# A two-layer kernel whose second layer follows the first at a distance of three units in place of two

## The chip, the cores and the metric

The kernel runs on one core of one Trainium2 chip. The metric is the device time of one execution in microseconds (us). The kernel before was run three times: 2016.63 us median, from 2016.15 to 2020.16. The profiled execution took 2016.63 us, and its trace spans 2014.8 us from the first to the last instruction.

The engines, by their names in the rows: PE is TensorE (matrix products; PEld its weight loads), DVE is VectorE, ACT is ScalarE, SP is SyncE, which here only issues transfers (its queue is SPq). Each engine takes its own instructions strictly in the order in which the program lists them and holds the next one until its semaphores allow it.

## The reference

For 2 sequences of 6080 steps and 256 channels, a gated scan, then two feed-forward blocks on the 12160 resulting rows:

```
f = lb + (1 - lb) * sigmoid(f_logit);  h = f * h + (1 - f) * x;  y[t] = h
z   = relu(y @ w_in1) ** 2 @ w_out1          # 256 -> 2048 -> 256
out = elu(z @ w_in2) @ w_out2                # 256 -> 2048 -> 256
```

The four weight matrices arrive as 64-bit floats.

## The kernel before

**Units.** The 12160 rows are cut into 12 units: unit 0 of 512 + 384 rows, all others of 512 + 512 (`units_of`). Each unit goes through the first layer (scan, `w_in1`, relu and square, `w_out1`) and, later, through the second (`w_in2`, elu, `w_out2`). The first layer's result of a unit goes to a buffer in HBM (`xd`) and is loaded back as `F1` when the second layer takes the unit up.

**Order of the units.** Lines 229 to 232 write down the list `runs` of (layer, unit). With `BEHIND = 2` it is (0,0) (0,1) (1,0) (0,2) (1,1) (0,3) ... (1,9) (0,11) (1,10) (1,11), with layer 0 for the first and 1 for the second. A stage, below, is one entry of this list.

**Slots.** A stage has 8 slots, one for each eighth of the hidden width. All products are made of three matmuls on a split of each number into a high and a low part (function `three`). In units 0 and 1 of the first layer (the "plain" stages) the two halves of the rows take 16 slots of 12 matmuls for `w_in` (into c0 and c1 or c2 and c3, by turns) and 12 for `w_out`. All other stages save an eighth of the first product by sums of blocks: a slot has 9 matmuls ("first", on tile `xa`), 12 ("later", on tile `xb`) and twice 12 for `w_out` ("out", L858), 45 in all. Each out needs one tile `g`, whose low part is the DVE instruction L681. So L681 comes 16 times in each stage, and counts the slots on DVE; the out that uses a `g` is issued some 8 us of planned time after its slot. L681 number 17 to 32 belong to (0,1), 33 to 48 to the third stage.

**What must stand before a stage.** (0,u) needs its rows scanned: in four quarters, each with loads of `fs` and `xs` (SP, L569, four issues each, two buffers each), one ACT instruction (L573), and on DVE two transposes (L578), two L584, L592, two scans (L605) and L610. The result is tile `F0`, one buffer. Then `add_parts` makes `xa` and `xb` (one buffer each) from `F0`, or from `F1` for the second layer, with L518 and L485, L488.

**Weights.** During the first two or three stages DVE and ACT also turn the 64-bit weights into high and low parts. `make` prepares a slot of `w_in` (for the second layer with four sums L319 to L322 and L342 and stores to `wd`), `out` a slot of `w_out`, and `sums` (`add_sums`) reloads a slot of `w_in1` from `rd` (SP, L455, tile `a<-rd`) and makes the sums that the 45-matmul slots of the first layer need. Their planned times are spread by lines 932 to 936: `make` and `out` of the second layer up to the start of (1,0), `sums` up to the start of (0,2).

**Order of instructions.** The class `Order` collects all steps with a cost in us and a due time, runs a list scheduler on these planned costs, and issues each engine's instructions in the resulting order. So the order on every engine is fixed when the program is built.

Of the kernel before, what the change touches and what calls it, by code (L numbers as in the profile page):

```python
# [18 lines left out]
SIZES = ((512, 384), (512, 512))  # L19
LEAD = 2  # L20
GAP = 56
BEHIND = 2
AGE = 8.0
ROW = 1 / 2240
START = 12.0
# [126 lines left out]
def kernel(  # L152
# [66 lines left out]
    def slots_of(m, u):  # L219

        if not plain(m, u):
            return [(m, u, None, g) for g in range(KG)]
        a, b = ([(m, u, h, g) for g in range(KG)] for h in range(2))
        got = a[:LEAD]
        for i in range(LEAD, KG + LEAD):
            got += a[i : i + 1] + b[i - LEAD : i - LEAD + 1]
        return got

    runs = [(0, u) for u in range(BEHIND)]
    for u in range(BEHIND, NU):  # L230
        runs += [(1, u - BEHIND), (0, u)]
    runs += [(1, u) for u in range(NU - BEHIND, NU)]
    slots = [s for r in runs for s in slots_of(*r)]
# [729 lines left out]
    for kind, s in pe_order:  # L963
# [4 lines left out]
        if kind != "later" and s == first_of[m, u]:  # L968
            if m == 0:
                keys = {}  # L970
                before = slots_of(0, u - 1)
                for hh in range(2):
                    due = in_due[(m, u, hh, 0) if plain(m, u) else s]
                    for q in range(2):
                        k = before[SCANS[2 * hh + q] * len(before) // KG] if u >= BEHIND else None
                        keys[hh, q] = add_scan(n_scan, u, hh, q, due - 6.0 + 2.0 * (q - 1), n_first[k] if k else None)
# [43 lines left out]
```

## Time and profile before

| | |
|---|---|
| median of 3 runs | 2016.63 us |
| profiled execution, its span | 2016.63 us, 2014.8 us |
| PE, DVE, ACT busy | 97%, 83%, 81% of the span |
| PE idle, waiting for `xa` | 35.0 us in 2 waits (one is the start of the program) |
| stages in the trace: (0,1) ends, (1,0) from and to, (0,2) begins in earnest | 181.57; 181.57 to 261.63; 282.77 us |

A row of the timeline has start and duration in us, the engine, the line, the tiles written and read, the count, and in brackets the idle time before it with what ended it. "x9" is nine instructions merged to one row.

### The profile page before, as it was taken

To read this page: it belongs to the slowest core of one execution; us is meant where nothing else is said; L and a number is where in the kernel's file an instruction comes from. 1 tells how busy PE (TensorE), PEld (TensorE's weight loads), DVE (VectorE), ACT (ScalarE), POOL (GpSimd) and SP (SyncE) were. 2 spreads that over 40 slices of the span, in tenths; PEclk is the share of its full clock that TensorE was granted. 3 is DMA by queue.
4 is the path that set the end of the run, shared out by engine and by line. 5 is a ranking of instruction groups with operands and counts; after the bars stand their busy time and mean duration, and the time that the engine had idled before them with its cause. 6 is when DMAs were issued, how large, how long until landed. Compare 5 with 4: busy or idle time off the path is not lost.

```text
span 2014.8 us, 24509 instructions
## 1 busy us (share of the span) xinstructions
PE 1964.0 (97%) x8688; PEld 1630.8 (81%) x8688; DVE 1674.3 (83%) x2285; ACT 1638.0 (81%) x2170; POOL 0.2 (0%) x4
## 2 busy tenths in 40 slices
PE   5999969999999999999999999999999999999998
PEld 4987958888888888888888888888888888888886
DVE  7877998888889879879888888987987988857886
ACT  6987968888888888888788788888888878878886
POOL 0000000000000000000000000000000000000000
PEclk9999989999999999999999999999999999999999
DMA  7877644324424334333432442433433333233231
GB/s 202 241 243 244 215 138 138 128 85 144 133 102 144 102 134 133 113 134 108 139 132 85 138 130 101 144 102 134 133 113 134 113 113 133 92 108 116 100 109 57
DMA packets 235138, 267.30 MB, mean 133 GB/s; under 512 B 160008, under 2 KB 160776, under 8 KB 235016
## 3 DMA queue, kind: packets, MB, share of 16 engines
q1 hardware_dynamic: 234432, 265.21, 41.3%
q8 instruction: 68, 1.11, 0.2%
q10 hardware_dynamic: 584, 0.53, 0.1%
q14 instruction: 54, 0.44, 0.1%
HBM read 221.91 MB, written 43.78 MB: 132 GB/s over the span
## 4 chain that ended last, share of the span: by engine, by line
PE 88%; DVE 4%; ACT 3%; DMA 2%; issue 1%; SPq 1%; ACTq 0%; DVEq 0%
PE a L858 47%; PE c L636 41%; DVE g L681 1%; DMA a<-rd 1%; DMA fs<-in_f_logit_dram 1%; ACT g L676 1%; ACT r L728 1%; ACT r L661 1%; SPq L569 0%; ACT a L372 0%; DVE a L378 0%; ACT st L375 0%; DVE a L381 0%; DMA st<-in_moe_w_in_dram 0%; DVE F L605 0%
## 5 line engine op out<-in xcount | busy, mean ns | idle before, releaser
L858 PE MATMUL a<-g,wo 128*128 128x512 f32 (+1 forms) x4608 | 1098.6, 387 | 0.9 <-DVE g L681 0.9
L858 PEld LDWEIGHTS a<-g,wo 128*128 128x128 f32 x4608 | 864.8, 188 | 173.8 <-DVE g L681 1.3
L681 DVE TENSOR_TENSOR g<-r,g 128x1024 fp32r<-128x1024 f32 (+2 forms) x384 | 463.4, 1207 | 157.5 <-ACT g L676 156.7
L636 PE MATMUL c<-xb,ws 128*128 128x512 f32 (+2 forms) x2208 | 525.7, 387 | 0.0
L676 ACT ACTIVATE g<-r 128x1024 fp32r<-128x1024 f32 (+2 forms) x384 | 403.4, 1051 | 110.0 <-PE a L858 91.6
L636 PEld LDWEIGHTS c<-xb,ws 128*128 128x128 f32 x2208 | 413.9, 188 | 82.2
L636 PE MATMUL c<-xa,ws 128*128 128x512 f32 (+1 forms) x1680 | 419.3, 393 | 43.0 <-ACT xa L485 35.0
L636 PEld LDWEIGHTS c<-xa,ws 128*128 128x128 f32 x1680 | 316.9, 190 | 114.6 <-ACT xa L485 35.4
L759 ACT ACTIVATE s<-c 128x512 f32<-128x512 f32 (+1 forms) x528 | 306.4, 586 | 5.5 <-PE c L636 4.7
L671 DVE SCALAR_TENSOR_TENSOR r<-e,r 128x1024 f32<-128x1024 f32 (+1 forms) x192 | 232.2, 1209 | 32.2 <-ACT e L668 32.1
L665 ACT ACTIVATE e<-r 128x1024 f32<-128x1024 f32 (+1 forms) x192 | 201.7, 1050 | 44.3 <-DVE r L803 41.4
L661 ACT ACTIVATE r<-r 128x1024 f32<-128x1024 f32 x192 | 201.6, 1050 | 2.4
L668 ACT ACTIVATE e<-e 128x1024 f32<-128x1024 f32 (+1 forms) x192 | 201.4, 1049 | 1.5
L799 ACT ACTIVATE r<-c 128x512 f32<-128x512 f32 (+1 forms) x176 | 104.0, 591 | 94.7 <-PE c L636 94.7
L763 DVE TENSOR_TENSOR s<-s 128x512 f32<-128x512 f32 (+1 forms) x176 | 119.9, 681 | 71.0 <-ACT s L759 70.9
L796 DVE TENSOR_TENSOR s<-c,s 128x512 f32<-128x512 f32 (+1 forms) x176 | 120.5, 685 | 27.1 <-PE c L636 24.5
L807 DVE TENSOR_TENSOR r<-c,s 128x512 f32<-128x512 f32 (+1 forms) x176 | 119.7, 680 | 4.4
L803 DVE TENSOR_TENSOR r<-c,s 128x512 f32<-128x512 f32 (+1 forms) x176 | 120.0, 682 | 2.2
L810 DVE TENSOR_TENSOR r<-s 128x512 f32<-128x512 f32 (+1 forms) x176 | 119.5, 679 | 0.0
L655 ACT ACTIVATE r<-r 128x1024 f32<-128x1024 f32 x80 | 84.3, 1054 | 3.8 <-DVE r L810 3.8
L658 ACT ACTIVATE r<-r 128x512 f32<-128x512 f32 x80 | 50.4, 630 | 35.8 <-DVE r L803 35.0
L605 DVE TENSOR_TENSOR_SCAN F<-fT,carry,xT 128x256 f32<-128x256 f32 (+2 forms) x94 | 65.4, 724 | 1.2
(47 smaller groups left out, 759.0 us busy)
## 6 DMA issues: line engine op xcount, KB each, us to landing
ws<-wd SPq DMA_DIRECT2D x176, 896.0 KB, 4.9
fs<-in_f_logit_dram SPq DMA_DIRECT2D x184, 64.0 KB, 2.1
xs<-in_x_dram SPq DMA_DIRECT2D x184, 64.0 KB, 2.2
xd<-o SPq DMA_DIRECT2D x46, 256.0 KB, 4.4
F<-xd SPq DMA_DIRECT2D x22, 512.0 KB, 4.6
out_dram<-o SPq DMA_DIRECT2D x88, 128.0 KB, 2.3
st<-in_moe_w_out_dram SPq DMA_DIRECT2D x16, 512.0 KB, 5.6
wd<-wp SPq DMA_DIRECT2D x24, 256.0 KB, 3.5
```

Of the source, the lines that this page charges most:

```text
L636: nc.tensor.matmul(out, lhsT=ws[:, p, w], rhs=xs[:, r, v], start=start and q == 0, stop=stop and q == 2, skip_group_check=check,)
L661: nc.scalar.activation(r_t[0], r_t[0], AF.Square)
L665: nc.scalar.activation(t["e"], r_t[0], AF.Relu, scale=-1.0)
L668: nc.scalar.activation(t["e"], t["e"], AF.Exp, scale=-1.0)
L671: nc.vector.scalar_tensor_tensor(r_t[0], t["e"], 1.0, r_t[0], op0=ALU.subtract, op1=ALU.max)
L676: nc.scalar.activation(g_t[s, which][:, 0], r_t[0], AF.Copy)
L681: nc.vector.tensor_tensor(g_t[s, which][:, 1], r_t[0], g_t[s, which][:, 0].bitcast(F32), op=ALU.subtract)
L759: nc.scalar.activation(t["s"][:, c - 1], t[c], AF.Copy)
L763: nc.vector.tensor_tensor(t["s"][:, 1], t["s"][:, 1], t["s"][:, 2], op=ALU.add)
L796: nc.vector.tensor_tensor(t["s"][:, 0], t[0], t["s"][:, 0], op=ALU.add)
L803: nc.vector.tensor_tensor(odd[0][:, 1], t[2], t["s"][:, 0], op=ALU.add)
L858: nc.tensor.matmul(a, lhsT=y, rhs=v, start=begin and jj == 0 and p == 0, stop=end and jj == len(mine) - 1 and p == 2, skip_group_check=True,)
```

## The change

One number. With `BEHIND = 3` the list `runs` is (0,0) (0,1) (0,2) (1,0) (0,3) (1,1) ... (0,11) (1,9) (1,10) (1,11).

```
-BEHIND = 2
+BEHIND = 3
```

All else follows from the planner. The scans of unit 2 and the `sums` of the first layer now have to stand before the third stage, which is (0,2); the second layer's weights have until the fourth. The condition `u >= BEHIND` at L975 drops the hold that tied the scans of unit 2 to slots of unit 1. The tiles' sizes and the filler tile of `GAP` = 56 floats ahead of the weight buffers are the same in both kernels. The number of instructions on each engine is the same.

On DVE, the kernel before ends the scan of unit 2 (tile F0_2514) here, between the L681 number 45 and 46 (g_2656, g_2663) of (1,0):

```order
L584 TENSOR_SCALAR fT_2665<-fT_2665,ga_59,gb_60 128x256
L681 TENSOR_TENSOR g_2656<-r_2519,g_2656 128x2x448
L584 TENSOR_SCALAR fT_2665<-fT_2665,ga_59,gb_60 128x256
L807 TENSOR_TENSOR r_2683<-c3_2565,s_2555 128x448
L592 SCALAR_TENSOR_TENSOR xT_2661<-fT_2665,xT_2661 128x512
L810 TENSOR_TENSOR r_2683<-s_2555 128x448
L605 SCALAR_TENSOR_TENSOR F0_2514<-fT_2665,carry_61,xT_2661 128x256
L681 TENSOR_TENSOR g_2663<-r_2549,g_2663 128x2x448
L605 SCALAR_TENSOR_TENSOR F0_2514<-fT_2665,carry_61,xT_2661 128x256
L671 SCALAR_TENSOR_TENSOR r_2645<-e_2659,r_2645 128x2x448
L610 COPY carry_61<-F0_2514 128x2
L518 TENSOR_TENSOR F0_2514<-F0_2514 128x512
```

The changed kernel ends the same scan (tile F0_1548) around L681 number 26 (g_1708) of (0,1):

```order
L578 STREAM_TRANSPOSE xT_1684<-xs_1624 128x8x2x32
L578 STREAM_TRANSPOSE fT_1695<-fs_1602 128x8x2x32
L610 COPY carry_61<-F0_1548 128x2
L584 TENSOR_SCALAR fT_1695<-fT_1695,ga_59,gb_60 128x256 x2
L592 SCALAR_TENSOR_TENSOR xT_1684<-fT_1695,xT_1684 128x512
L605 SCALAR_TENSOR_TENSOR F0_1548<-fT_1695,carry_61,xT_1684 128x256
L681 TENSOR_TENSOR g_1708<-r_1575,g_1708 128x1024
L378 SCALAR_TENSOR_TENSOR a_1711<-a_1711,st_1658 128x512
L605 SCALAR_TENSOR_TENSOR F0_1548<-fT_1695,carry_61,xT_1684 128x256
L381 SCALAR_TENSOR_TENSOR a_1711<-st_1658,a_1711 128x512
L610 COPY carry_61<-F0_1548 128x2
L518 TENSOR_TENSOR F0_1548<-F0_1548 128x512
```

In the first list the scan's end stands beside L681 number 46, that is at the 14th of 16 slots of its stage, in the second at the 10th.

On SP, the loads of unit 2 stand before the change among the weight loads (L475) of (1,0), with reloads from `rd` and `xd` between them:

```order
L569 DMA xs_2476<-in_x_dram 32x8x64 x4
L455 DMA a_2496<-rd6_168 128x512
L918 DMA F1_2390<-xd1_171 128x1024
L475 DMA ws_2525<-wd0_0_146 128x2x896
L569 DMA fs_2559<-in_f_logit_dram 32x8x64 x4
L569 DMA xs_2580<-in_x_dram 32x8x64 x4
L475 DMA ws_2622<-wd0_1_147 128x2x896
L569 DMA fs_2640<-in_f_logit_dram 32x8x64 x4
```

After the change they stand among the stores of weights (L345, L346) and the reloads for `sums` of (0,1):

```order
L569 DMA xs_1424<-in_x_dram 32x8x64 x4
L472 DMA ws_1449<-wd0_6_152 128x2x512
L345 DMA wd0_3_149<-wp_1438 128x512
L346 DMA wd0_3_149<-a_1419 128x512
L569 DMA fs_1478<-in_f_logit_dram 32x8x64 x4
L569 DMA xs_1502<-in_x_dram 32x8x64 x4
L455 DMA a_1524<-rd4_166 128x512
L569 DMA xs_1527<-in_x_dram 32x8x64 x4
L345 DMA wd1_2_156<-wp_1517 128x512
L346 DMA wd1_2_156<-a_1466 128x512
L345 DMA wd1_2_156<-wp_1546 128x512
L346 DMA wd1_2_156<-a_1519 128x512
```

A load behind an L345 or L346 is not issued before DVE or ACT has made what that store takes.

## Rows read from the trace of the kernel before

**Rows 1.** The page: the span, busy times, granted clock in 40 slices.
```profile
span 2014.8 us, 24509 instructions
PE 1964.0 (97%) x8688; PEld 1630.8 (81%) x8688; DVE 1674.3 (83%) x2285; ACT 1638.0 (81%) x2170; POOL 0.2 (0%) x4
PEclk9999989999999999999999999999999999999999
```

**Rows 2.** Timeline of PE where (0,2) begins.
```profile
261.63 0.40 PE L636 MATMUL c<-xa,ws 128*128 128x512 f32 x1
...
278.23 0.79 PE L636 MATMUL c<-xa,ws 128*128 128x512 f32 x1 [15.13 <-ACT xa L485]
280.48 2.50 PE L636 MATMUL c<-xa,ws 128*128 128x512 f32 x5 [1.46 <-DVE xa L488]
282.77 3.10 PE L858 MATMUL a<-g,wo 128*128 128x448 f32 x12
285.71 2.91 PE L636 MATMUL c<-xb,ws 128*128 128x512 f32 x12
```

**Rows 3.** Two stretches of DVE: length, busy (count), clock, DMA share, GB/s.
```profile
107.87:164.42 56.55, 41.42 (x76) 1.00 0.77 243
182.04:280.34 98.30, 93.45 (x154) 0.91 0.61 187
```

**Rows 4.** Groups of DVE in 182.04:280.34: busy, mean ns of one, idle before.
```profile
L681 DVE TENSOR_TENSOR g<-r,g 128x896 fp32r<-128x896 f32 (+1 forms) x17 | 18.8, 1105 | 0.0
L319 DVE TENSOR_TENSOR a<-a 128x128 f32<-128x128 f32 x4 | 1.2, 289 | 3.8 <-DMA a<-rd 3.8
```

**Rows 5.** Timeline of DVE, a scan and what follows it at once.
```profile
263.36 0.74 DVE L605 TENSOR_TENSOR_SCAN F<-fT,carry,xT 128x256 f32<-128x256 f32 x1
264.02 1.06 DVE L671 SCALAR_TENSOR_TENSOR r<-e,r 128x896 f32<-128x896 f32 x1
```

**Rows 6.** Timeline of PE, two slots apart by 45 matmuls in (1,1).
```profile
361.76 2.20 PE L636 MATMUL c<-xa,ws 128*128 128x512 f32 x9
...
371.96 2.20 PE L636 MATMUL c<-xa,ws 128*128 128x512 f32 x9
```

**Rows 7.** Timeline of PE from (0,1) to (1,0).
```profile
178.85 2.88 PE L858 MATMUL a<-g,wo 128*128 128x512 f32 x12
181.57 0.77 PE L636 MATMUL c<-xa,ws 128*128 128x448 f32 x3
...
185.31 1.49 PE L636 MATMUL c<-xa,ws 128*128 128x448 f32 x3 [1.55 <-ACT r L728]
186.60 3.73 PE L858 MATMUL a<-g,wo 128*128 128x512 f32 x12
...
204.07 2.90 PE L858 MATMUL a<-g,wo 128*128 128x512 f32 x12
206.81 1.99 PE L636 MATMUL c<-xa,ws 128*128 128x448 f32 x9
...
215.93 1.99 PE L636 MATMUL c<-xa,ws 128*128 128x448 f32 x9
```

**Rows 8.** Timeline of DVE: L681 number 22 and 28.
```profile
141.65 1.23 DVE L681 TENSOR_TENSOR g<-r,g 128x1024 fp32r<-128x1024 f32 x1 [1.30 <-ACT g L676]
...
173.63 1.22 DVE L681 TENSOR_TENSOR g<-r,g 128x1024 fp32r<-128x1024 f32 x1
```

**Rows 9.** Waits of DVE for the reloads of `sums`.
```profile
DVE a L319 <- DMA a<-rd: 11.2, 5, 3.8
```

**Rows 10.** Page, DMA issues: KB each and median us to landing; all packets.
```profile
DMA packets 235138, 267.30 MB, mean 133 GB/s; under 512 B 160008, under 2 KB 160776, under 8 KB 235016
fs<-in_f_logit_dram SPq DMA_DIRECT2D x184, 64.0 KB, 2.1
```

**Rows 11.** Chain of waits: start, us, a load of `fs` in it.
```profile
261.29 4.63 DMA fs<-in_f_logit_dram
```

**Rows 12.** Stage (0,1), all engines: length, PE, PEld, DVE, ACT, POOL, clock, DMA.
```profile
94.50:181.57 87.07, 87.07 (x396) 73.34 (x394) 67.64 (x123) 72.64 (x113) 0.00 (x0) 1.00 0.79 257
```

## The prediction

> **What bounds the kernel now.** I read the page first: PE is busy for 97% of the span and its clock is at full speed in all slices but one [rows 1]. So the time is PE's work plus the few places where PE has none, and a change of order can only act there. The timeline of PE shows two such places after the start of the program. From 282.77 us to the end I leave it alone: every stage transition there is an old one of the kind that the changed kernel has as well, and at (1,1) PE goes over without a gap [rows 6].
>
> The large gap is at the start of (0,2) [rows 2]. PE begins its nine "first" matmuls at 261.63 and issues the next out at 282.77. A slot of 45 matmuls of 512 columns takes 371.96 - 361.76 = 10.20 us [rows 6], 0.227 each, so nine take 2.04, and the out should start at 263.67: 19.1 us are lost. After it the twelve matmuls from 282.77 to 285.71 take 2.94 where twelve take 2.72, and five of the first ones took 2.50, half speed; with what that slowed out adds (at 448 columns it should have taken 2.43) the loss is 19.6 us. The wait is for `xa`, that is for the scans of unit 2.
>
> The small one is from (0,1) to (1,0) [rows 7]: from the first matmul at 181.57 to the out at 204.07 there are two firsts and two laters of 448 columns and three outs of 512. At 9.12 us for a slot of 448 (215.93 - 206.81) this is 16.7 us in place of 22.5: 5.8 us lost, most of it to waits for ACT and to matmuls that run slower behind them.
>
> Why is `xa` late for (0,2)? DVE. From 182.04, where it writes `xb` of (1,0), to 280.34, where `xa` of (0,2) is done, it is busy for 93.45 of 98.30 us [rows 3]: it is full, and PE has only 74.1 us of matmuls in (1,0) (8 x 9.12, and four outs of 512 columns still from the plain stage, 0.29 more each). So (1,0) asks DVE for more than PE lasts, and the difference is the gap.
>
> **The change, step by step.** I count the instructions of DVE between fixed points of its list in both kernels, and price each kind by its mean in the trace, less 0.08 us, since in a full queue the next one starts before the recorded end: L605 has 0.74 and its successor starts 0.66 later [rows 5]. The means are L681 1.105, L319 0.289 and so on [rows 4].
>
> Check on before: from `xb` of (1,0) to `xa` of (0,2) its list has 151 instructions: 17 L681 (17.6 us), 16 L671 (16.0), 40 L763 to L810 (21.1), the 32 of unit 2's scans (15.5: per quarter two transposes 1.22, two L584 0.66, L592 0.60, two L605 1.32, L610 0.07), 39 for weights (15.2) and 7 for parts (5.6). Sum 91.0, where 93.45 were measured as busy. So the counting is good to some 3%.
>
> Now the changed kernel by stages:
> - (0,1), from `xb` of unit 1 to the last of `xa` for (0,2): 109 instructions, 55.7 us (12 L681 13.5, scans 32 15.5, weights 59 22.0, parts 6 4.7). In the trace the first point is at 107.87 and PE wants (0,2) at 181.57: 73.7 us. In the part of it up to 164.42 DVE was busy for 41.42 of 56.55 [rows 3], and the list gains 15.5 of scans there and loses 6.7 of weights.
> - (0,2), from `xb` of (0,2) to `xb` of (1,0): 143 instructions, 82.2 us (16 L681 18.3, 39 of L763 to L810 23.6, weights 63 25.0, scans 14 7.0, parts 11 8.3). PE has 8 x 10.20 = 81.6.
> - (1,0), to `xb` of (0,3): 103 instructions, 69.1 us, for 74.1 of PE.
>
> Nothing disappears: scans and weights are the same number of instructions. But the work with an early due time is now spread over three stages, each about as long as PE's, where before one stage of 74.1 us had to hold 91. `xa` and `xb` of each next stage stand before L681 number 13 and 14 of the stage under way, while (0,2) had its `xb` done only beside number 15 and 16.
>
> *The term that goes*: -19.6.
>
> *The transition out of (0,1)* stays one, now to (0,2). PE's list is the same in form, c1 to c3 are released by the same late relus on ACT, and DVE makes the same kind of parts. Its price lies between 0 (as at (1,1), rows 6) and the 21.1 us of [rows 2]; nearest is the 5.8 it costs today [rows 7], so nothing changes: +0.
>
> *A jam inside (0,1).* The four quarters stand between L681 number 22 and 28. These six intervals hold 33.7 us of DVE work; the trace gives them 173.63 - 141.65 = 31.98 [rows 8]. That is 1.7 late, and one reload for `sums` stands in it on which DVE waits: five such waits took 11.2 us, 3.8 the longest [rows 9], none at the least. With the mean, 2.2, number 28 is 3.9 late. Its out is issued at 178.85 [rows 7], 4.0 after the L681 ends. So PE just does not notice; at 3.8 it would lose 1.5. I take +0.5.
>
> *(0,2) itself* is full on DVE: 82.2 against 81.6. Three reloads stand in it, at 0 to 3.8 us each. When DVE lags behind, the reload is issued earlier against it and the wait shrinks: in 182.04:280.34, also full, there is one of 3.8 before four sets of sums [rows 4]. The parts have about 5 us before PE wants them: in before, DVE starts L681 number 28 five us ahead of its out. I take +0.5 as what is left over, with 0 and 11.4 as the ends.
>
> *(1,0)* has 5 us of room, so +0. ACT is busy for 72.64 of the 87.07 us of (0,1) [rows 12], and gives up weight steps there and gets four tanh; no term. At the end three second-layer stages follow one another in place of two; the one more transition from second layer to second layer costs between 0 [rows 6] and 5.8 [rows 7]; DVE has no scans to do there, so I take +0.
>
> Sum: 2016.63 - 19.6 + 0.5 + 0.5 = 1998.0. The profiled execution took just the median, 2016.63, so no correction is needed; I forecast 1998.
>
> *A rule that speaks against it.* The loads of `fs` and `xs` are issued in pieces of 64 KB that land after 2.1 us in the median, and most packets of the run are under 512 B [rows 10]; in the chain of waits one load took 4.63 [rows 11]. The change puts all sixteen of unit 2's groups into (0,1), where the DMA share is 0.79 [rows 12]. The Trainium skill, "DMA: Bandwidth & Descriptors", section Specifications, gives 512 B as the smallest transfer that runs at line rate. By it these loads would stretch in the busiest stage, and the sum would be that of the third rival; by the median of the row they land in time and the sum stands. The one slow landing here is in the rule's sense, the median is not; no row shows such loads all through a stage at 0.79.
>
> **Rivals.**
> 1. *A second jam at (1,0).* The three reloads and the 0.6 us of overload are not hidden: 3 x 3.8 + 0.6 = 12.0, less 5 of room, is 7.0 lost before (1,0): 2016.63 - 19.6 + 0.5 + 7.0 = 2004.5. For it: DVE has no reserve in (0,2). Against: a full DVE waited once in 98 us [rows 4].
> 2. *The gap moves.* `xa` of (0,2) is as late for the third stage as for the fourth: the 19.6 are paid at 181.57, and the time is 2016.6, the same. For it: all of the scan is now due 80 us of PE earlier. Against: 55.7 us of DVE work in 73.7.
> 3. *Scans behind the stores: slower.* SP issues a quarter's loads behind L345 and L346, which wait for DVE, and DVE's transposes wait for the loads, with every L681 queued behind them. If each of the eight transposes waits a full landing of 4.63 [rows 11], DVE stands for 37.0 us. Of this 15.1 fit into what was idle up to 164.42 less the 8.8 that the list gains, so 6.3, and 4.0 into the out's lead: 26.7 lost for 19.6 won, 2016.63 + 7.1 = 2023.7. It is slower from 3.7 us a transpose on ((19.6 + 10.3) / 8). For it: the order of SP and the share of 0.79. Against: two buffers each, so a quarter's loads stand one quarter ahead.
> 4. *All smooth.* The 5.8 go too, as at (1,1): 2016.63 - 25.4 = 1991.2. It needs ACT to be free at the transition, where its list still holds weight steps.
>
> **How the numbers follow.** Forecast 0.68, rival 1 0.14, rival 2 0.06, rival 3 0.07, rival 4 0.05. A measurement of this kernel tells differences of about 0.2%, 4 us, from none. Faster by more: forecast, rivals 1 and 4, 0.87. Within: most of rival 2, 0.05. Slower: rival 3 and a little of 2, 0.08. The range leaves out rivals 2, 3 and the best of 4: 1992 to 2007.
>
> **What would show it.** Right: PE without a wait over 5 us after its first matmul, the second layer's (1,0) begun some 88 us after the end of (0,1), and DVE over 95% busy from about 140 to 265 us. The jam in (0,1): L858 waiting for L681 between 150 and 182. Rival 1: PE waiting for L485 or L488 near 265 to 280. Rival 3: DVE waiting for `fs` or `xs` at L578. What would make the forecast wrong is above all a DVE that stands still where my sum has it full, since no list here leaves it more than 5 us to catch up.

## The result and the profile after

The changed kernel took 2000.61 us, the median of 4 executions (1999.9 to 2001.33), against 2017.27 us (2016.15 to 2020.16) for the kernel before in the same comparison: a ratio of 0.9916 with the interval 0.9904 to 0.9928. It is faster by 16.7 us, where 18.6 were forecast. The profiled execution took 2000.24 us, 16.4 less than that of before. The page, for [rows 1]:

```profile
span 1998.4 us, 24516 instructions
PE 1963.1 (98%) x8688; PEld 1628.9 (82%) x8688; DVE 1674.6 (84%) x2291; ACT 1633.3 (82%) x2164; POOL 0.2 (0%) x4
PEclk9999999999999999999999999999999999999999
```

The busy times of PE and DVE are those of before within 1 us; the span is 16.4 shorter. So what went is idle time, and the slice with the lower clock went with it. The waits of PE in the changed kernel (in all, how often, the longest):

```profile
PE c L636 <- ACT xa L485: 19.6, 1, 19.6
PE c L636 <- ACT ws L407: 2.7, 1, 2.7
PE c L636 <- ACT r L728: 2.3, 1, 2.3
PE c L636 <- DVE r L807: 1.2, 2, 0.7
PE a L858 <- DVE g L681: 1.0, 2, 0.9
PE c L636 <- DVE xa L488: 0.9, 1, 0.9
PE c L636 <- ACT r L799: 0.2, 1, 0.2
```

The rows for `xa` and L407 belong to the start of the program, and the L858 wait of 0.9 to its last slot, where the kernel before has the same; no wait for `xa` is left after the start [rows 2]. The timeline of PE from (0,1) into (0,2) answers [rows 7]:

```profile
175.41 2.79 PE L858 MATMUL a<-g,wo 128*128 128x512 f32 x11 [0.17 <-DVE g L681]
...
183.64 0.84 PE L636 MATMUL c<-xa,ws 128*128 128x512 f32 x3
186.74 2.02 PE L636 MATMUL c<-xa,ws 128*128 128x512 f32 x6 [2.26 <-ACT r L728]
...
207.22 2.20 PE L636 MATMUL c<-xa,ws 128*128 128x512 f32 x9
...
217.42 2.20 PE L636 MATMUL c<-xa,ws 128*128 128x512 f32 x9
```

Stage (0,2) begins at 183.64, 2.07 later than the third stage of the kernel before, (1,0), began there. From 183.64 to 207.22 are two slots, 20.4 us of matmuls, in 23.6: the transition costs 3.2. After it every slot takes 10.20 until (1,0), which is the next place where PE loses time:

```profile
268.42 1.37 PE L636 MATMUL c<-xa,ws 128*128 128x448 f32 x6
270.29 0.88 PE L636 MATMUL c<-xa,ws 128*128 128x448 f32 x3 [0.49 <-DVE r L807]
...
299.92 0.88 PE L636 MATMUL c<-xa,ws 128*128 128x448 f32 x3 [0.72 <-DVE r L807]
...
345.68 2.34 PE L636 MATMUL c<-xa,ws 128*128 128x512 f32 x9 [0.24 <-ACT r L799]
```

From 268.42 to 345.68 are 77.3 us, where the prediction counts 74.1 of matmuls: 3.2 lost. The three waits shown are 1.45 of it, some 0.8 are slots of 448 columns that took longer without a wait (last section), and the rest is matmuls that took longer around the waits. The stretches of DVE (length, busy with the count, clock, DMA share, GB/s), in the order (0,1), whose first stretch is that of [rows 3], then (0,2), then the first half of (1,0):

```profile
107.87:164.42 56.55, 44.34 (x85) 1.00 0.75 225
185.70:268.62 82.92, 81.54 (x143) 1.00 0.76 238
268.62:302.86 34.24, 34.24 (x55) 1.00 0.60 192
```

DVE's 41.42 of before became 44.34 in the first row. In (0,2) it is busy for 98%, and for 34 us after that it never stops at all.

With the starts of the stages on PE the whole difference can be set out (us; "again" is a second profile of the same changed kernel, the last two columns are experiments below):

| from, to | before | after | again | weights 30 before | weights at (0,2) |
|---|---|---|---|---|---|
| 0, start of (0,1) | 96.2 | 97.0 | 97.4 | 96.2 | 97.2 |
| (0,1) | 85.4 | 86.7 | 87.0 | 87.8 | 85.4 |
| third stage | 80.1 (1,0) | 84.8 (0,2) | 84.7 | 82.9 | 84.5 |
| fourth stage | 100.1 (0,2) | 77.3 (1,0) | 76.6 | 76.3 | 77.4 |
| two slots of the fifth stage | 20.4 (1,1) | 19.4 (0,3) | 19.4 | 19.4 | 19.5 |
| from there to the last slot | 1603.85 | 1603.83 | 1603.87 | 1603.87 | 1603.87 |
| start of the last slot to the end | 28.8 | 29.5 | 29.5 | 28.9 | 29.0 |

The stretch of [rows 12] begins 1.7 us ahead of (0,1); the stage itself took 85.4. Four outs behind each (1,0) still have 448 columns, so the stage that follows it is 1.2 shorter: (0,2) before, the fifth after. From the third slot of the fifth stage to the last slot of the program, 157 slots, the kernels agree within 0.05 us. All that the change wins lies before 385 us. Behind the last slot's start it loses 0.7, after the last matmul, in both of its profiles; why, no run here shows.

### The profile page after: what moved, and what is told of

The parts are those of the page before. It is cut to its first block, busy times and chain, and to the rows that moved or that the text cites. A ratio compares the mean times of both kernels' runs of the same rounds, so it can differ in the third digit from the quotient of the medians.

```text
span 1998.4 us, 24516 instructions
## 1 busy us (share of the span) xinstructions
PE 1963.1 (98%) x8688; PEld 1628.9 (82%) x8688; DVE 1674.6 (84%) x2291; ACT 1633.3 (82%) x2164; POOL 0.2 (0%) x4
## 4 chain that ended last, share of the span: by engine, by line
PE 91%; DVE 5%; DMA 1%; ACT 1%; issue 1%; SPq 1%; DVEq 0%; ACTq 0%
PE a L858 48%; PE c L636 43%; DVE g L681 1%; DVE a L342 1%; SPq L569 0%; DMA fs<-in_f_logit_dram 0%; DMA a<-rd 0%; DMA xs<-in_x_dram 0%; ACT g L676 0%; DMA st<-in_moe_w_in_dram 0%; DVE a L378 0%; DVE a L381 0%; DVE fT L578 0%; DVE F L605 0%; DVE s L763 0%
## 5 line engine op out<-in xcount | busy, mean ns | idle before, releaser
L858 PE MATMUL a<-g,wo 128*128 128x512 f32 (+1 forms) x4608 | 1099.0, 387 | 1.2 <-DVE g L681 1.0
L858 PEld LDWEIGHTS a<-g,wo 128*128 128x128 f32 x4608 | 863.3, 188 | 175.5 <-DVE g L681 3.1
L681 DVE TENSOR_TENSOR g<-r,g 128x1024 fp32r<-128x1024 f32 (+2 forms) x384 | 463.0, 1206 | 153.6 <-ACT g L676 152.0
L636 PE MATMUL c<-xa,ws 128*128 128x512 f32 (+1 forms) x1680 | 417.7, 392 | 27.1 <-ACT xa L485 19.6
L636 PEld LDWEIGHTS c<-xa,ws 128*128 128x128 f32 x1680 | 316.4, 189 | 98.2 <-ACT xa L485 19.6
L671 DVE SCALAR_TENSOR_TENSOR r<-e,r 128x1024 f32<-128x1024 f32 (+1 forms) x192 | 232.1, 1209 | 29.9 <-ACT e L668 29.9
L799 ACT ACTIVATE r<-c 128x512 f32<-128x512 f32 (+1 forms) x176 | 104.2, 592 | 82.6 <-PE c L636 82.1
L807 DVE TENSOR_TENSOR r<-c,s 128x512 f32<-128x512 f32 (+1 forms) x176 | 119.3, 678 | 4.5 <-DVE g L681 0.5
```

The lines of the kernel that those rows point to most:

```text
L636: nc.tensor.matmul(out, lhsT=ws[:, p, w], rhs=xs[:, r, v], start=start and q == 0, stop=stop and q == 2, skip_group_check=check,)
L671: nc.vector.scalar_tensor_tensor(r_t[0], t["e"], 1.0, r_t[0], op0=ALU.subtract, op1=ALU.max)
L681: nc.vector.tensor_tensor(g_t[s, which][:, 1], r_t[0], g_t[s, which][:, 0].bitcast(F32), op=ALU.subtract)
L858: nc.tensor.matmul(a, lhsT=y, rhs=v, start=begin and jj == 0 and p == 0, stop=end and jj == len(mine) - 1 and p == 2, skip_group_check=True,)
```

## The experiments

**The same kernel again, and with its hold restored.** The diff has a second effect by L975, the hold on the scans of unit 2; this puts it back.

```
-k = before[...] if u >= BEHIND else None
+k = before[...] if u >= 2 else None
```

> The changed kernel with the one other thing undone that its constant does: the scans of unit 2 are held again to slots of unit 1 (L975). The list of DVE then differs in small: the last quarter's scans stand at L681 number 25 to 27 in place of 25 and 26, and xa of (0,2) before number 29 in place of 28. Theory (the order of stages and the due times do it, the hold is nothing): 1999 to 2003, at most 2 us for a later xa. Rival (dropping the hold is what brings unit 2's scans forward): a gap at the start of (0,2) of 10 us or more, 2009 to 2017.

One execution: 2000.25 us, a span of 1998.5. The changed kernel as it is, run beside it:

> The changed kernel itself, to stand beside the two with later weights: 1998.5 to 2001.5 by every theory.

2000.5 us (1999.5 to 2000.99), ratio 0.992 [0.9905, 0.9935]. So the hold is worth nothing here, and the effect is the order of the stages, with the due times that follow from it.

**The scans earlier, the order of the stages as before.** Is `xa` late because the scans are due late, or because DVE has no time for them? In the kernel before, the scans of unit 2 get a due time 30 us earlier and no hold.

```
-k = ... if u >= BEHIND else None
-... add_scan(..., due - 6.0 + 2.0 * (q - 1), ...)
+k = ... if u >= 3 else None
+... add_scan(..., due - (36.0 if u == 2 else 6.0) + 2.0 * (q - 1), ...)
```

> The kernel before (two units behind), with one edit: the scans of unit 2 are due 30 us earlier, so that on DVE they stand beside L681 number 35 to 38 of (1,0) in place of 42 to 46, and xa of (0,2) before number 45. What makes room is that weight steps and elu stand later. Theory (DVE is full in (1,0): 91 us of listed work for 74.1 of PE): the order cannot help much, the work pushed back has to be done before or in (0,2) all the same; some 15.2 of the 91 are weights that can wait for (0,2), so at best 15 us of the 19.6 come back, and new waits of PE for DVE or ACT show inside (1,0). About 2005 to 2015. Rival (the gap is a matter of due times alone, not of a full DVE): the gap goes whole and nothing takes its place, 1998 to 2001, as fast as three units behind.

2011.03 us (8 executions), ratio 0.9973 [0.9963, 0.9983]: 5.7 of the 16 us. The timeline of PE in (1,0) and at the start of (0,2) of this kernel:

```profile
229.16 0.87 PE L636 MATMUL c<-xa,ws 128*128 128x448 f32 x3 [1.85 <-DVE r L807]
...
236.45 0.47 PE L858 MATMUL a<-g,wo 128*128 128x448 f32 x1 [1.54 <-ACT g L676]
240.56 4.47 PE L858 MATMUL a<-g,wo 128*128 128x448 f32 x11 [3.64 <-DVE g L681]
245.73 0.74 PE L636 MATMUL c<-xa,ws 128*128 128x448 f32 x1 [0.70 <-ACT r L799]
...
275.19 1.54 PE L636 MATMUL c<-xa,ws 128*128 128x512 f32 x6
```

The gap at the start of (0,2) is gone, but (1,0), begun at 182.5, now takes 92.7 us in place of 80.1. The scans, moved ahead, push the L681 and L807 of (1,0) back, and PE waits for those. DVE has no idle time there (length, busy with the count, clock, DMA share, GB/s):

```profile
215.00:245.70 30.70, 30.67 (x56) 0.89 0.82 257
```

That is the theory of a full DVE; a late due time alone is refuted. That late loads hold the scans back, as [rows 11] might suggest, does not fit the kernel before either: while PE stands in its gap, DVE works through (length, PE, PEld, DVE, ACT, POOL busy, clock, DMA).

```profile
261.63:282.77 21.14, 4.21 (x10) 2.40 (x9) 21.11 (x38) 10.68 (x15) 0.00 (x0) 0.62 0.38 101
```

**More work on DVE, in both kernels.** If (0,2) and (1,0) now have room, work added there is partly free; if DVE has none, it is paid in full. Each set of the four sums L319 to L322 is made three times (two needless repeats, 1.88 us for each of the 16 sets, at both places where the sums are made; later lines shift by up to 4, so L681 reads L685, L728 reads L732 and L858 reads L862).

```
 weight_sums(t["q"], t["a"])
+weight_sums(t["q"], t["a"])
+weight_sums(t["q"], t["a"])
```

On the changed kernel:

> The changed kernel, with each set of four sums of weights (L319 to L322) done three times over in place of once, in the same place of the list: 1.88 us more per set (four steps of 0.21, 0.21, 0.32, 0.20, twice). Three sets stand between L681 number 22 and 28, six in (0,2). Theory (DVE has about 4 to 5 us of room in each of these and no more): (0,1) loses some 5 us more before (0,2), and (0,2) some 11.3 - 4 = 7 before (1,0): about 2012. Rival (DVE only waits, it has work for much less than the stage): the added work goes into the waits, 2001 to 2004.

On the kernel before:

> The kernel before with the same tripled sums. Four sets (7.5 us) stand between xb of (1,0) and xa of (0,2), eight in (0,1), where DVE was idle for 15 us of 56. Theory (the gap is DVE's work in (1,0)): the gap grows one for one, from 19.6 to about 27, and (0,1) loses 0 to 3: 2024 to 2028. Rival (the gap is a chain of loads and waits): it grows by less than 3, 2017 to 2020.

One execution each: 2026.03 us, 25.4 above the changed kernel, and 2043.13, 26.4 above the kernel before beside it (2016.73). The theories, about 2012 and 2024 to 2028, were far too low, and the rivals lower still: above all they priced (0,1) too low, which became 14.2 longer where 5 were expected, and 11.4 where 0 to 3 were. The waits of the changed kernel with more sums in (0,1), on the timeline of PE:

```profile
110.61 3.89 PE L862 MATMUL a<-g,wo 128*128 128x384 f32 x11 [4.15 <-DVE g L685]
...
165.77 4.92 PE L862 MATMUL a<-g,wo 128*128 128x512 f32 x11 [4.31 <-DVE g L685]
```

And its whole stretch (0,1) (length, PE, PEld, DVE, ACT, POOL busy, clock, DMA):

```profile
97.30:198.10 100.80, 91.59 (x385) 74.98 (x385) 91.16 (x218) 68.47 (x104) 0.00 (x0) 0.93 0.64 205
```

The same stretch of the changed kernel:

```profile
97.00:183.60 86.60, 86.28 (x385) 71.28 (x384) 73.04 (x140) 66.83 (x103) 0.00 (x0) 1.00 0.75 238
```

DVE had 86.60 - 73.04 = 13.6 us idle in (0,1). It got 18.1 more work, and the stage became 14.2 longer: the idle time took up 3.9 of it. Of the 14.2, 5.3 is PE itself, busy for 91.59 in place of 86.28 for the same matmuls at a granted clock of 0.93. I had counted the idle time of DVE as room; in the changed kernel 8.1 us of it are waits of DVE for ACT and 3.5 for reloads, and the work was added elsewhere in the list. In front of the two late L685 shown, DVE is busy for 13.13 of 13.30 us (97.3 to 110.6) and for 11.43 of 11.64 (154.06 to 165.7), while 9.6 us of idle time stay in the rest of the stage. In (0,2) six sets add 11.3 us, and (0,2) and (1,0) become 8.8 and 2.4 longer, together one for one. In the kernel before, six sets fall between the start of (1,0) and the second slot of (0,2), which grows by 13.6. The loss came at another place than I expected, though: the gap did not grow (21.2 us from the first matmul of (0,2) to the next out, against 21.1), and PE waited more at the start of (1,0):

```profile
199.61 1.49 PE L640 MATMUL c<-xa,ws 128*128 128x448 f32 x3 [4.57 <-ACT r L732]
```

So DVE's work is paid in full in the third and fourth stages of both kernels: the change moved work to where it cost less, but left no reserve. These are single executions, but 25 us is far beyond the 4 us that executions of the kernel before differ by.

**Four behind.** The same number once more.

```
-BEHIND = 2
+BEHIND = 4
```

> The changed kernel with four units behind in place of three: (0,0) (0,1) (0,2) (0,3) (1,0) ... The second layer's weights have one more stage. Theory (work with an early due time, spread over more PE time, fits): no gap over 3 us at any transition, and the 3.1 us that (1,0) still loses in the changed kernel, where PE waits for L807 of a late DVE, go: 1996 to 2000. Rival (three is enough, what is left is not DVE's load): same as the changed kernel within 2 us, 1999 to 2002. Second rival (four second-layer stages in a row at the end cost something): 2002 to 2006.

2005.36 us (2002.95 to 2005.91, 4 executions), ratio 0.9941 [0.9924, 0.9957]: slower than three, and my 1996 to 2000 missed it, as did the first rival. The second rival had the number but put it in the tail; the loss is early. Here (0,2) is followed by (0,3), and PE waits at that transition:

```profile
272.55 1.52 PE L636 MATMUL c<-xa,ws 128*128 128x512 f32 x6
276.75 0.98 PE L636 MATMUL c<-xa,ws 128*128 128x512 f32 x3 [2.68 <-DVE r L807]
277.57 4.50 PE L858 MATMUL a<-g,wo 128*128 128x512 f32 x12
```

This slot takes 14.83 us in place of 10.20. Besides, (0,1) takes 89.3 us where three behind has 86.7, and (0,2) 86.3 where it has 84.8; (1,0) loses 0.6 where it lost 3.2, so that part of the theory held. With four, unit 3's scans stand almost whole in (0,2) (14.3 us of DVE in the trace, where the changed kernel has 7.0), with 2.4 us more for the parts of the next stage, and only 4.4 us of weight work leaves the same part of the list: between L681 number 30 and 46 it has 85.1 us of work by the prediction's prices, 80.0 with three, for 81.6 of PE.

**The second layer's weights later.** With three behind, the second layer starts 87 us later, but `make` and `out` of its weights are still spread from the start of (0,1) on. The changed kernel with their spread begun 30 us ahead of (0,2):

```
+T9 = in_due[first_of[0, 2]] - 30.0
-weights.append((T0 + (T1 - T0) * (g + 0.5) / KG, "make", 1, g, None))
-weights.append((T0 + (T2 - T0) * (g + 1) / KG, "out", 1, g, None))
+weights.append((T9 + (T1 - T9) * (g + 0.5) / KG, "make", 1, g, None))
+weights.append((T9 + (T2 - T9) * (g + 1) / KG, "out", 1, g, None))
```

> The changed kernel; the planned times of the second layer's weights (make and out) are spread from 30 us before (0,2) on, in place of from the start of (0,1). Counted from the list, in the changed kernel and here: L681 number 22 to 28 hold 33.6 and 32.3 us of DVE work, number 30 to 46, (0,2), 80.0 and 74.1, number 46 to 62, (1,0), 72.2 and 76.0. Theory (what a stage loses is DVE work over PE time in that stretch): (0,1) keeps about its 1.3 us, (0,2) stays smooth, and (1,0), where DVE starts some 5 us less behind, loses 1 to 3: 1997.5 to 2000.5, at most 3 us better than the changed kernel. Rival (weights pushed later become late for (1,0)): a wait of PE for second-layer weights, over 2002.

1997.19 us (1996.77 to 1998.87), ratio 0.9906 [0.989, 0.9923], beside 2000.5 for the changed kernel on the same chip, and no execution of either falls into the other's span. It is the fastest version, just below my 1997.5 to 2000.5. Begun right at (0,2) (without the 30.0):

> The same with the second layer's weights spread from the start of (0,2) on. L681 number 12 to 22 hold 46.5 us of DVE work (38.9 in the changed kernel), since the scans of unit 2 come forward to number 18 to 21; 22 to 28 hold 26.1 (33.6); 30 to 46 84.8 (80.0); 46 to 62 70.1 (72.2). Theory: the 1.3 us that (0,1) lost at its end go, but (0,2) has 84.8 for 81.6 of PE and loses 2 to 4 by waits for L807, as four units behind did: 2000 to 2003. Rival (only the order within (0,1) matters): 1998 to 1999.5.

1999.06 us (1997.6 to 1999.76), ratio 0.9913 [0.9898, 0.9927]. My theory's 2000 to 2003 missed; the rival's number holds. By the table, later weights at (0,2) free (0,1), 85.4 as before, and cost 1.4 in the middle of (0,2), where a slot takes 11.16: the jam I expected there exists but is small. What both versions win is the transition into (0,2). The timeline of ACT at this place in the changed kernel:

```profile
184.09 0.61 ACT L337 ACTIVATE wp<-a 128x512 fp32r<-128x512 f32 x1
184.61 0.65 ACT L372 ACTIVATE a<-st 128x512 f32<-128x512 f32 x1
185.17 1.04 ACT L485 ACTIVATE xb<-F 128x1024 fp32r<-128x1024 f32 x1
186.11 0.57 ACT L728 ACTIVATE r<-c 128x512 f32<-128x512 f32 x1
```

The same with the weights begun 30 us ahead:

```profile
183.85 1.04 ACT L485 ACTIVATE xb<-F 128x1024 fp32r<-128x1024 f32 x1
185.23 1.09 ACT L728 ACTIVATE r<-c 128x512 f32<-128x512 f32 x2 [0.34 <-DVE g L681]
```

The L728 that empties the bank stands behind two weight steps (L337, L372) in the first and behind none in the second, and PE's wait for it is 1.05 instead of 2.26, as its timeline has it:

```profile
183.99 0.84 PE L636 MATMUL c<-xa,ws 128*128 128x512 f32 x3
185.88 1.65 PE L636 MATMUL c<-xa,ws 128*128 128x512 f32 x6 [1.05 <-ACT r L728]
```

From 183.99 the two slots take 21.7 in place of 23.6. Of the 2.9 us between the two profiles' spans this is 1.8, and (0,1) gives 1.1 back. The rest is 0.8 at the start of the program, where two profiles of the changed kernel differ by 0.5, 0.9 in (1,0), where they differ by 0.7, and 0.6 behind the last slot; none of it is traced to the edit.

## Why the prediction was right, point by point

- *The term that goes, -19.6.* Right. No wait of PE for `xa` is left after the start, and the second experiment shows why: with the same scans due earlier but (1,0) still third, two thirds of the loss only moved into (1,0). The reason given, that (1,0) asks DVE for more than PE lasts, stands; the price of added sums in the kernel before, 13.6 us for 11.3, is a second witness.
- *The transition out of (0,1), 5.8 as before, +0.* Too high by 2.6: it costs 3.2. Now there is one wait, 2.26 for L728, where before had 1.55 [rows 7] and three short ones of 0.55, 0.21 and 0.99, 3.3 in all. So 1.0 of the 2.6 is in the waits; the other 1.6 is matmuls, which before ran at a granted clock of 0.50 behind the 1.55, and which now kept the full one (last section):

```profile
185.31:186.80 1.49, 1.49 (x4) 0.50 0.42 78
```

  The profile with the hold restored has a wait of 2.22 here and a granted clock of 0.50 behind it, and its two slots lose 4.0: the size of this term depends in part on luck. What the wait consists of is as rival 4 had it: weight steps on ACT.
- *A jam in (0,1), +0.5.* Larger, and in part elsewhere: (0,1) takes 86.7 against 85.4, +1.3, in the second profile +1.7. In the first, 1.0 of it is outs between 150 and 182 that start late or stretch, among them one counted wait for L681, of 0.17: the place is right there, L681 behind the scans. In the second, 1.2 of it stands at one earlier out, ahead of the scans' jam:

```profile
106.94 2.20 PE L858 MATMUL a<-g,wo 128*128 128x384 f32 x11 [0.97 <-DVE g L681]
```

  The waits for the reloads fell over the whole program from 11.2 in 5 [rows 9], which may have helped:

```profile
DVE a L319 <- DMA a<-rd: 5.2, 4, 1.6
```

- *(0,2) full on DVE, +0.5.* DVE was busy for 81.54 us where I had counted 82.2, and PE lost nothing inside the stage. The lag comes out one stage later.
- *(1,0) has 5 us of room, +0.* Wrong, and the largest miss: 3.2 us (2.5 in the second profile), of which 1.8 to 1.9 lie in the two slots with a wait for L807, 0.4 to 0.5 at the wait for L799, and some 0.8 in the first profile's slower slots. The step that failed is "the parts have about 5 us before PE wants them". That is true of parts and of L681, but not of L807, which empties a bank that PE writes again a few matmuls later. And the room in (1,0), 69.1 us of DVE for 74.1 of PE, is room of the whole stage: in its first 34 us, where both waits lie, DVE had none. The list of DVE at the second of these waits:

```profile
296.11 0.61 DVE L803 TENSOR_TENSOR r<-c,s 128x448 f32<-128x448 f32 x1
296.65 1.08 DVE L671 SCALAR_TENSOR_TENSOR r<-e,r 128x896 f32<-128x896 f32 x1
297.65 1.08 DVE L681 TENSOR_TENSOR g<-r,g 128x896 fp32r<-128x896 f32 x1
298.65 0.68 DVE L592 SCALAR_TENSOR_TENSOR xT<-fT,xT 128x512 f32<-128x512 f32 x1
299.25 0.61 DVE L807 TENSOR_TENSOR r<-c,s 128x448 f32<-128x448 f32 x1
```

  Between the two instructions that empty banks stand 2.6 us of an L671, an L681 and a step of unit 3's scan, without a gap, and PE, from 297.81 on at its first products, waits for the last. Rival 1 had its size at 7.0 and its wait at L485 and L488: its cause, no reserve on DVE in (0,2), was right, its place and size were not.
- *Rival 3* did not come. DVE has no wait for `fs` or `xs` at L578 after the start of the program (7.4 us, once); a single wait of 1.2 at L378, ahead of (0,1), names a load of `fs`. The Trainium skill ("DMA: Bandwidth & Descriptors", Specifications) gives 512 B as the smallest transfer at line rate, which by the prediction's reading would have made these loads late; at a DMA share of 0.75 in (0,1), the trace of the changed kernel shows no wait of DVE for one of them.
- *The tail, +0.* Right up to the last slot, 1603.83 against 1603.85 us; the end behind it is 0.7 longer.
- *The signs.* DVE is busy for 119.92 of the 125 us from 140 to 265, 96%, as said; (1,0) begins 84.8 after the end of (0,1), not 88, since the transition cost less.

The sum with the measured terms, for the profiled executions: -19.6 for the gap, -2.6 for the transition, +1.3 in (0,1), +3.2 in (1,0), +0.2 in the slots behind its wait for L799 and +0.7 at the start of the program is -16.8. The last slot starts 17.1 earlier (the 0.3 are slots that differ by 0.2 or less), and with the 0.7 behind it the span is 16.4 shorter. The mechanism of the large term was right; that the sum came within 2.2 us, in profiled time, owes something to luck, since the errors of the terms cancelled in part: the forecast was too high by 2.6 at the transition and by 0.5 for (0,2), and too low by 0.8 in (0,1), 3.2 in (1,0), 0.2 behind it, 0.7 at the start and 0.7 at the end. The 0.7 at the start stands in the wait for L407 at 31 us (2.7, before it was 2.0), ahead of about 79 us, the first place where the lists differ; it is not the change's.

## What to carry to other kernels

Count the work of an in-order engine between fixed points of its list and compare it with what the bound engine lasts there: that found the gap and its cure (18.6 us forecast, 16.7 measured). Do not count the engine's idle time as room, though (18 us of added work used 4 of 14 idle us). Give each step the lead that it has itself: here the lead of L681 was taken for that of L807, which empties a bank, and (1,0) lost its time there. When a stage moves, try the due times of the work that was spread to meet it: a version with those moved was 3.3 us faster, of which 1.8 are traced to the transition.

## What the runs showed that I had not expected

A wait of PE can cost more than itself. In the kernel with four behind PE waited 2.68 us, and the twelve matmuls of the next out took 4.50 us in place of 2.88. The granted clock there (length, PE busy, clock, DMA):

```profile
272.55:277.57 5.02, 2.34 (x10) 1.00 0.37 151
277.57:282.07 4.50, 4.50 (x14) 0.62 0.01 4
```

In the changed kernel, behind the wait of 2.26, the clock was still granted in full:

```profile
186.74:188.76 2.02, 1.93 (x7) 1.00 0.85 226
```

And in the changed kernel with more sums, behind its wait of 4.15 us:

```profile
110.61:114.46 3.85, 3.85 (x12) 0.50 0.37 134
```

There the eleven matmuls ran at 0.50, the lower of the two levels, 1.2 GHz. The length of the wait alone does not decide it. With the hold restored, the same place as in the changed kernel has a wait of 2.22 and the lower level behind it:

```profile
186.83:189.76 2.93, 2.93 (x7) 0.50 0.63 180
```

In the kernel before, the lower level already came behind 1.55, with a wait of 0.55 shortly ahead of it. What else decides, these runs do not show. Where the clock falls, what comes behind the wait can cost about as much as a short wait does: 1.6 us behind the 2.68, and 1.7 behind the 4.15.

Slots of 448 columns took 9.30 us in (1,0) of the changed kernel's first profile and 9.12 in its second, from 308 to 336 us of the first, both at a granted clock of 1.00 and with no wait of PE. The cause is open; with the parts of slots next to them it is some 0.8 us, and the list of PE is the same in both.
